# One first load of 65 KiB a row in two descriptors, in place of loads of 8 and 57 KiB: x + alpha * fx

## The chip, the cores and the metric

The kernel runs on one core of one Trainium2 chip. The metric is device time in microseconds, as the median of repeated runs; the kernel before takes 151.0 us (three runs, 150.94 to 151.18). A separate execution is recorded by the hardware profiler, and all views of the profile tell of that one.

## The reference

```python
B, S, D = 512, 32, 640            # all bf16; alpha has one element
def reference(x, fx, alpha):
    return x + alpha * fx
```

Two tensors of 20 MiB (20.97 MB) are read, one of the same size is written. Per element there is one multiply and one add.

## The kernel before, in words

**Tiling.** Each tensor is seen as 128 partition rows of 160 KiB (`ROW = 160`, in units of `K = 512` bf16 elements, which are 1 KiB). All work is told in KiB of a row: "x 0 64" is the first 64 KiB of each of the 128 rows. On the chip there is one flat buffer `t`, 128 partitions of 160 + 47.5 KiB. x lies in it at its own place, 0 to 160, and the result overwrites x there. There is not room for all of fx beside it: fx passes through places that are free for a while, the part of x's own space that has not been loaded yet (95 to 160) and the spare 47.5 KiB (160 to 207.5).

**The steps.** `PLAN` (lines 27 to 54) is the order of work, written out by hand, one step to a line; nothing reorders it. There are these kinds:

- `x a b` loads x from a to b (`load_x`, line 96), `f a b p` loads fx from a to b into place p (`load_f`, line 100), `a` loads alpha (`load_alpha`, lines 103 to 110), `s a b` stores the result (`store`, line 119). All of these are issued by SyncE (SP), into one DMA queue that the 16 DMA engines work off in order.
- `m a b` multiplies fx by alpha in place on VectorE (DVE) (line 113), and `c a b` adds it to x (line 116), also on DVE.

Alpha is loaded into eight partitions; a matmul with a row of ones (line 108) spreads one of them over 128 partitions, and DVE copies it from PSUM to `a_f` (line 110), which all multiplies read.

**What sets the order around the change.** Each engine does its own steps in the order of `PLAN`. Between engines, semaphores carry the data's dependencies: a multiply waits for its fx load, an add for its x load, a load into a place waits until what lay there has been used. So the load "x 95 160" (line 39) is issued only when the adds on fx 0 to 65, which lies in 95 to 160, are over; "f 112.5 142.5" and "f 142.5 160" wait in the same way for the adds over 65 to 95 and 95 to 112.5. The first store is held until "m 112.5 134.5" is over (line 47), and the others follow the adds. A last instruction of SP waits for all but the last store.

**Descriptors.** A load of 128 rows becomes one packet for each contiguous piece of a row, eight rows to each of the 16 DMA engines. Rows of 8, 57, 64, 31, 47.5, 30 and 17.5 KiB go in one piece; the rows of 65 KiB of "x 95 160" go in two of 32.5 KiB (128x2x16640 elements).

Of the kernel before, what the change touches and what calls it, by code (L numbers as in the profile page):

```python
# [1 line left out]

# [4 lines left out]

ALU = mybir.AluOpType
F32 = mybir.dt.float32

P = 128
K = 512
ROW = 160
SPARE = 47.5

LANES = 8

PLAN = """
f 0 8 95
a
f 8 65 103  # L30
x 0 64
x 64 95
f 65 112.5 160
m 0 8
m 8 65
c 0 8
c 8 64
c 64 65
x 95 160
m 65 95  # L40
c 65 95
f 112.5 142.5 160
m 95 112.5
c 95 112.5
f 142.5 160 190
m 112.5 134.5
s 0 64 | m 112.5 134.5
m 134.5 142.5
c 112.5 142.5
m 142.5 160  # L50
c 142.5 160
s 64 128
s 128 160
"""


@with_exitstack
def kernel(
    ctx: ExitStack,
    tc: tile.TileContext,  # L60
    x: bass.AP,
    fx: bass.AP,
    alpha: bass.AP,
    out: bass.AP,
):
    nc = tc.nc
    xv, fv, ov = (
        t.flatten_outer_dims().rearrange("(p n) d -> p (n d)", p=P) for t in (x, fx, out)
    )
    assert xv.shape[1] == ROW * K  # L70

    consts = ctx.enter_context(tc.tile_pool(name="consts", bufs=1))
    psum = ctx.enter_context(tc.tile_pool(name="psum", bufs=1, space=bass.MemoryType.PSUM))
    flat = ctx.enter_context(tc.tile_pool(name="flat", bufs=1))
    ctx.enter_context(tc.manual_schedule())
    t = flat.tile([P, int((ROW + SPARE) * K)], x.dtype, name="t")
    info = mybir.DependencyInfo(mybir.DependencyClass.Sync, mybir.DependencyReason.DATA)

    lanes = {}
    lies = []  # L80
    done = []

    def at(a, b):
        return t[:, int(a * K) : int(b * K)]

    def of(v, a, b):
        return v[:, int(a * K) : int(b * K)]

    def place(a, b):
        for c, d, p in reversed(lies):  # L90
            if c <= a and b <= d:
                return at(p + a - c, p + b - c)
        raise ValueError(f"fx {a} to {b} lies nowhere in one piece")

    def load_x(a, b):
        done.append(nc.sync.dma_start(out=at(a, b), in_=of(xv, a, b)))

    def load_f(a, b, p):
        lies.append((a, b, p))
        done.append(nc.sync.dma_start(out=at(p, p + b - a), in_=of(fv, a, b)))  # L100

    def load_alpha():
        a_n = consts.tile([LANES, 1], alpha.dtype, name="a_n")
        done.append(nc.sync.dma_start(out=a_n[:], in_=alpha[None, :].to_broadcast([LANES, 1])))  # L104
        ones = consts.tile([1, P], alpha.dtype, name="ones")
        nc.vector.memset(ones[:], 1.0)  # L106
        a_ps = psum.tile([P, 1], F32, name="a_ps")
        done.append(nc.tensor.matmul(a_ps[:], ones[:], a_n[0:1, :], start=True, stop=True))  # L108
        lanes["a"] = consts.tile([P, 1], F32, name="a_f")
        nc.vector.tensor_copy(out=lanes["a"][:], in_=a_ps[:])  # L110

    def multiply(a, b):
        done.append(nc.vector.tensor_scalar_mul(place(a, b), place(a, b), lanes["a"][:]))  # L113

    def add(a, b):
        done.append(nc.vector.tensor_add(at(a, b), at(a, b), place(a, b)))  # L116

    def store(a, b):
        done.append(nc.sync.dma_start(out=of(ov, a, b), in_=at(a, b)))

    does = {"x": load_x, "f": load_f, "a": load_alpha, "m": multiply, "c": add, "s": store}
    begun = {}
    for step in filter(None, PLAN.split("\n")):
        step, *later = step.split(" | ")
        what, *numbers = step.split()
        does[what](*map(float, numbers))
        begun[step] = done[-1]
        for other in later:
            tc.add_manual_dep(done[-1].ins, begun[other].ins.name, info, reason="begins late")

    rest = nc.sync.nop(nofuse=True)
    for i in done[:-1]:
        tc.add_manual_dep(rest.ins, i.ins.name, info, reason="all but the last store")


# [1 line left out]
_INS = ['x', 'fx', 'alpha']  # L137
_OUTS = [((512, 32, 640), 'bfloat16')]


# [23 lines left out]
```

## Time and profile before

| | |
|---|---|
| median of 3 runs | 151.0 us (150.94 to 151.18) |
| the profiled execution's own time | 151.11 us |
| its span, first to last instruction | 149.3 us |
| DMA queue | 1728 packets, 62.92 MB, 98.0% of 16 engines |
| mean rate over the span | 421 GB/s |
| DVE busy | 66.5 us (45%), 16 instructions |
| adds (line 116) | 43.6 us in 7 |
| multiplies (line 113) | 22.8 us in 7 |
| DVE idle ahead of multiplies, waiting for fx | 25.7 us in 3 waits, the longest 15.3 |
| DVE idle ahead of adds, waiting for x | 16.5 us in 2 waits, the longest 11.6 |

How to read it: "busy" is the time in which an engine works, and the idle time of an engine that is not the bottleneck costs nothing. The DMA share of the queue is the mean over the 16 DMA engines. In the chain of waits each step is followed back to what released it; "another core or an unknown queue" is a release that the profile could not put a name to. A landing is the moment at which a transfer's completion is seen by the engine that waits for it. In the windows a packet is counted whole in the window in which it starts, so a short window can show a share over 1.

### The profile page before, as it was taken

What the parts mean: (1) busy time and instruction counts of PE and PEld (TensorE: products, weight loads), DVE (VectorE), ACT (ScalarE), POOL (GpSimd) and SP (SyncE); (2) the same over time, 40 slices, a digit from 0 to 9 for tenths busy, and PEclk for the clock granted to TensorE, in tenths of its full rate; (3) what the DMA queues carried; (4) which work ended last, traced back from release to release, by engine and by line L of the source; (5) the groups of instructions that cost most, each with busy time, mean ns of one, the idle gap of its engine ahead of it and who ended that gap; (6) DMA issues with size and microseconds to landing.
All of it is one profiled execution on the core that took longest, in us unless ns stands there. A gap on an engine that the chain in (4) does not pass through costs nothing.

```text
span 149.3 us, 84 instructions
## 1 busy us (share of the span) xinstructions
PE 0.2 (0%) x1; PEld 0.1 (0%) x1; DVE 66.5 (45%) x16; POOL 0.2 (0%) x4
## 2 busy tenths in 40 slices
PE   0000000000000000000000000000000000000000
PEld 0000000000000000000000000000000000000000
DVE  0300008920069999029997093599997000000000
POOL 0000000000000000000000000000000000000000
DMA  5969998969699999999999999899896969697993
GB/s 147 603 281 500 500 461 351 562 281 562 281 408 451 438 417 443 456 429 428 428 428 428 417 444 469 378 526 492 351 562 281 562 281 562 281 562 307 456 474 167
DMA packets 1728, 62.92 MB, mean 421 GB/s; under 512 B 192, under 2 KB 192, under 8 KB 192
## 3 DMA queue, kind: packets, MB, share of 16 engines
q1 hardware_dynamic: 1728, 62.92, 98.0%
HBM read 41.94 MB, written 20.97 MB: 421 GB/s over the span
## 4 chain that ended last, share of the span: by engine, by line
DMA 38%; DVE 33%; another core or an unknown queue 4%; SPq 1%; issue 0%; DVEq 0%
DMA t<-in_x_dram 27%; DVE t L116 26%; DMA t<-in_fx_dram 11%; DVE t L113 7%; SPq L100 0%; SPq L104 0%; DVEq L116 0%
## 5 line engine op out<-in xcount | busy, mean ns | idle before, releaser
L116 DVE TENSOR_TENSOR t<-t 128x15360 bf16<-128x15360 bf16 (+4 forms) x7 | 43.6, 6252 | 16.6 <-DMA t<-in_x_dram 16.5
L113 DVE TENSOR_SCALAR t<-t,a_f 128x4096 bf16<-128x4096 bf16 (+4 forms) x7 | 22.8, 3265 | 25.7 <-DMA t<-in_fx_dram 25.7
L110 DVE COPY a_f<-a_ps 128x1 f32<-128x1 f32 x1 | 0.2, 159 | 5.2 <-PE a_ps L108 5.2
L106 DVE MEMSET ones<- 1x128 bf16 x1 | 0.2, 165 | 0.8 <-PEq L148 0.8
L108 PE MATMUL a_ps<-a_n,ones 1*128 1x1 bf16 x1 | 0.2, 158 | 6.0 <-DMA a_n<-in_alpha_dram 6.0
L148 POOL MEMSET const-bfloat16-1.0<- 128x1 bf16 x1 | 0.1, 102 | 0.0
L148 POOL MEMSET const-uint8-127<- 128x1 uint8 x1 | 0.1, 102 | 0.0
L148 POOL MEMSET const-float32-1.0<- 128x1 f32 x1 | 0.1, 99 | 0.0
L108 PEld LDWEIGHTS <-ones 1*128 1x128 bf16 x1 | 0.1, 98 | 1.0 <-DVE ones L106 1.0
L148 POOL MEMSET const-float32-0.0<- 128x1 f32 x1 | 0.1, 98 | 0.2 <-issue 0.2
## 6 DMA issues: line engine op xcount, KB each, us to landing
t<-in_x_dram SPq DMA_DIRECT2D x1, 8320.0 KB, 25.8
t<-in_fx_dram SPq DMA_DIRECT2D x1, 7296.0 KB, 21.4
t<-in_fx_dram SPq DMA_DIRECT2D x1, 6080.0 KB, 63.0
out_dram<-t SPq DMA_DIRECT2D x1, 4096.0 KB, 33.7
t<-in_x_dram SPq DMA_DIRECT2D x1, 3968.0 KB, 49.3
t<-in_fx_dram SPq DMA_DIRECT2D x1, 3840.0 KB, 16.4
t<-in_fx_dram SPq DMA_DIRECT2D x1, 2240.0 KB, 9.5
t<-in_fx_dram SPq DMA_DIRECT2D x1, 1024.0 KB, 5.0
```

The source lines that it names most:

```text
L106: nc.vector.memset(ones[:], 1.0)
L108: done.append(nc.tensor.matmul(a_ps[:], ones[:], a_n[0:1, :], start=True, stop=True))
L110: nc.vector.tensor_copy(out=lanes["a"][:], in_=a_ps[:])
L113: done.append(nc.vector.tensor_scalar_mul(place(a, b), place(a, b), lanes["a"][:]))
L116: done.append(nc.vector.tensor_add(at(a, b), at(a, b), place(a, b)))
L148: nc = _bacc.Bacc("TRN2", target_bir_lowering=False, num_devices=1)
```

## The change

Two loads of fx, the first 8 KiB of each row and then the next 57, become one load of 65 KiB a row. Such a row goes as two descriptors of 32.5 KiB, in the shape that "x 95 160" already has. It still lies at 95 to 160 of the buffer. There are seven loads of x and fx instead of eight. Alpha's load, which stood between the two, now follows the one. The multiplies over 0 to 8 and 8 to 65 become one over 0 to 65, and the adds over 0 to 8 and 8 to 64 one over 0 to 64; the add over 64 to 65 stays.

```diff
 PLAN = """
-f 0 8 95
+f 0 65 95
 a
-f 8 65 103
 x 0 64
 x 64 95
 f 65 112.5 160
-m 0 8
-m 8 65
-c 0 8
-c 8 64
+m 0 65
+c 0 64
 c 64 65
 x 95 160
 m 65 95
```

Nothing else differs. On each engine the remaining instructions stand in the same order: DVE has 14 in place of 16 (without its branches), SP one load fewer, and what later instructions wait for is the same data as before.

## The prediction

> **What bounds the kernel now.** I read the page's slices first, then the queue, the chain of waits, the timeline of VectorE (DVE), SyncE's (SP's) timeline, and last the windows over the first microseconds.
>
> ```profile
> DMA  5969998969699999999999999899896969697993
> q1 hardware_dynamic: 1728, 62.92, 98.0%
> ```
>
> The 16 DMA engines are busy for 98.0% of the span, and the dips in the slices are packets counted whole in the slice they start in. The bound is therefore bytes: 62.92 MB through 16 engines. The chain, in order of time:
>
> ```profile
> 1.59 0.35 SPq L100
> 1.94 0.04 issue
> 1.98 40.34 DMA t<-in_x_dram
> ...
> 42.41 17.63 DVE t L116 x3
> 60.04 6.08 another core or an unknown queue
> 66.12 0.02 issue
> 66.14 4.23 DVE t L113
> ```
>
> It runs through DVE from 42.41 to 60.04, but the 6.08 us behind that show that DVE did not set the pace there: the load issued at 60.07 was queued behind fx 65 to 112.5, which landed only at 66.12. What the reader is to see: queued loads land one behind the other without a hole. First multiplies and adds on DVE, whose starts are those landings, and SP's issues:
>
> ```profile
> 0.73 0.38 SPq L100 DMA_DIRECT2D t<-in_fx_dram  x1
> 5.97 0.16 PE L108 MATMUL a_ps<-a_n,ones 1*128 1x1 bf16 x1 [5.97 <-DMA a_n<-in_alpha_dram]
> 22.99 7.82 DVE L113 TENSOR_SCALAR t<-t,a_f 128x29184 bf16<-128x29184 bf16 x1 [15.34 <-DMA t<-in_fx_dram]
> 60.07 0.38 SPq L96 DMA_DIRECT2D t<-in_x_dram  x1
> 85.94 4.83 DVE L116 TENSOR_TENSOR t<-t 128x8960 bf16<-128x8960 bf16 x1 [4.91 <-DMA t<-in_x_dram]
> ```
>
> Only the start is not at full rate. Of these windows only the last two columns matter here, the DMA share and GB/s. A packet is counted whole where it starts, so GB/s over share is the rate of an engine while busy (times 16), and share times window times 16 is the packets' own time.
>
> ```profile
> 1.70:2.10 0.40, 0.00 (x0) 0.00 (x0) 0.00 (x0) 0.00 (x0) 1.00 2.08 287
> 2.10:2.30 0.20, 0.00 (x0) 0.00 (x0) 0.00 (x0) 0.00 (x0) 1.00 0.00 0
> 2.30:2.60 0.30, 0.00 (x0) 0.00 (x0) 0.00 (x0) 0.00 (x0) 1.00 0.15 55
> 3.40:4.80 1.40, 0.00 (x0) 0.00 (x0) 0.00 (x0) 0.00 (x0) 1.00 0.97 410
> 6.90:7.60 0.70, 0.00 (x0) 0.00 (x0) 0.70 (x1) 0.00 (x0) 1.00 3.08 1334
> 5.50:22.00 16.50, 0.16 (x1) 0.00 (x0) 1.45 (x2) 0.00 (x0) 1.00 0.91 396
> 66.00:84.50 18.50, 0.00 (x0) 0.00 (x0) 14.84 (x3) 0.00 (x0) 1.00 1.00 432
> ```
>
> In 1.70 to 2.10 start 287 x 0.40 = 115 KB, 14 packets of 8 KiB, of 2.08 x 0.40 x 16 / 14 = 0.95 us each; from 3.40 on one takes 0.31 us (8192 B at 410/0.97 = 423 GB/s over 16). So 14 engines begin at once and each loses some 0.64 us on its first packet; the other two begin only after 2.30. In 6.90 to 7.60 all 16 engines start a 57 KiB packet (1334 x 0.70 = 934 KB), each their second; one takes 58368 B at 396/0.91 = 435 GB/s, 2.15 us, so the first ones started between 4.75 and 5.45. Eight packets of 0.31 us from 1.75 on would have ended at 4.23: **the start costs each engine 0.5 to 1.2 us, and the kernel ends by the last engine.**
>
> **The change, part by part.** The profiled execution took 151.11 us, 1.8 around its span of 149.3, and is 0.11 above the median of 151.0.
>
> *Bytes and packets.* Per partition row 8 + 57 KiB become 32.5 + 32.5 KiB: the same bytes, and 256 descriptors either way. Before: 1.049 MB at 423 and 7.471 MB at 435 GB/s, 2.48 + 17.17 = 19.65 us. After: if the new row runs at the full 435, 8.520 MB take 19.59 (-0.07). The nearest row by shape is the load of x 95 to 160, two descriptors of 32.5 KiB too: 85.94 - 66.14 = 19.80 us (+0.15). That load ran beside 14.84 us of DVE work in 18.5 us; the first load will run beside none. I take 0, bounds -0.07 and +0.15.
>
> *One load fewer in the queue.* If a queued load had a fixed price, short ones would land late for their size. fx 112.5 to 142.5 (30 KiB a row) landed at 94.95, 9.01 after the one ahead, 0.300 us a KiB; x 0 to 64 took 42.32 - 22.99 = 19.33, 0.302 a KiB. The short one is not dearer, so in the queue the price is about nothing. Alone, a load does have one:
>
> ```profile
> t<-in_fx_dram SPq DMA_DIRECT2D x1, 1024.0 KB, 5.0
> ```
>
> The first load needs 5.0 us from issue to landing, 2.5 over the 2.48 of its bytes. I take 0, the queue's row, as every load but the first is queued; the bounds are 0 and -2.5. The Trainium skill, "DMA: Bandwidth & Descriptors", section "Anatomy of one DMA — SWDGE (gpsimd) path", fits a transfer as some 2.0 us fixed plus its bytes; by that figure, paid one behind the other, the sum would be 149.0. The section is for another issuing engine; the first load's row agrees with such a cost, the landings in the queue show it hidden.
>
> *SP.* One issue (0.35 us and 0.04 behind it) goes; alpha's stays at 1.17, and x 0 to 64, x 64 to 95 and fx 65 to 112.5 are issued 0.39 us sooner. The engines need x 0 to 64 only at about 22, so this is worth nothing.
>
> *Alpha, and DVE's multiplies.* Alpha's few bytes are now queued behind 65 instead of 8 KiB a row, so they land at about 23.0 and not 5.97. From alpha's landing to the first multiply it takes 6.36 - 5.97 = 0.39 us (matmul, copy). The two multiplies (1.29 + 7.82) become one of 33280 columns: 7.82 plus 4096 columns at (7.82 - 4.22)/(29184 - 15360) = 0.26 ns, 8.89 us. It starts at some 23.4 to 23.7 and ends by 32.6. Nothing else is queued behind it on DVE but the add that waits for x, landing at 42.32: 9.7 us of cover. If that were gone, each us would delay x 95 to 160, with the slack that comes next.
>
> *DVE's adds.* 2.29 + 15.09 become one of 32768 columns: 15.09 + 4096 x (15.09 - 8.16)/(28672 - 15360) = 17.22 us, 0.16 less. SP issues x 95 to 160 at about 59.9 and not 60.07. From SP's first issue at 0.73 to the first packets in the window from 1.70 are 1.0 us, so that the descriptors stand ready at 61, and the queue ahead lands at 66.12: some 4 us of slack, and the 0.16 us buys nothing. The later links (issues at 78.58, 90.79, 98.15) keep their distances, as they hang on landings.
>
> *The start itself.* The first packet of an engine is 32.5 KiB, not 8. Trace and kernel show no start of that shape. Best case: only the first packet's loss (0.64 us in the mean) is left, what the last engine lost on its next packets is covered, 1.2 - 0.64 = -0.56. Worst case: 16 descriptors for an engine instead of 8 take twice as long to come; the last engine began between 2.30 and 2.70 (0.6 to 0.95 behind the first), twice that is 1.2 to 1.9, against 1.2 lost now: up to +0.7. The nearest row is the same addresses' start, as all engines read the same first bytes of the same rows: I take 0.
>
> Sum: 0 + 0 + 0 on 151.11, less the 0.11 to the median: **151.0 us.**
>
> **The rivals.**
>
> *Faster: the ramp's later losses go (150.45).* Speaks for it: between 2.60 and the steady 0.31 us the engines still lose, and with 1.2 us of bytes in each packet an engine has its next descriptor long before it needs it. [...] 151.0 - 0.56 = 150.45.
>
> *Slower: descriptors come later (151.5).* Place: SP's first issue, with 256 descriptors ahead of the first byte of the last engines. For it: two of 16 engines began over 0.5 us behind the others, and the issues that follow rise from 0.35 to 0.51 us each, as if something behind SP were full. It decides once the last engine begins over 1.2 us behind the first, at about 2.95; doubled offsets give 0 to 0.7 more, in the middle 0.35, and with the +0.15 of the row rate 151.5. Against: the only such load took SP 0.38 us (60.07), as long as the first load of 128 descriptors. The Trainium skill, "Perfetto Trace Analysis", section "DMA Instruction — HWDGE (DVE, Sync)", puts the making of descriptors inside that time, and by it all would stand ready before the first packet; that leaves the time at 151.0.
>
> *No effect for another reason: DVE.* The late alpha takes the place of a wait; it decides only beyond 9.7 us. 151.0.
>
> *Much faster: each load pays the first one's 2.5 us (148.5).* 151.0 - 2.5, if the queue hid nothing of it. The landings in the queue, with no 2.5 us between a short and a long load, speak against it.
>
> **How the numbers follow.** This kernel's runs differ by 0.24 us, so 0.2% (0.3 us) is about what can be told from none. Forecast, no change, 0.48 (its own range 150.7 to 151.3); with the two-descriptor row at its worst, +0.15, 0.02; ramp gains 0.20; fixed cost 0.02; late descriptors 0.28. So faster 0.22, same 0.50, slower 0.28. The range goes from 150.4 (the ramp's gain in full) to 151.7 (+0.7 on the last engine).
>
> **What would show it.** Right: 14 or more engines begin at about 1.7 to 2.1, the add after fx 0 to 65 starts at 42.4 plus or minus 0.3, its multiply at 23.4 to 23.7, the last add and the last store keep their distance to it, and the span is 149.0 to 149.6. The faster rival shows as x 0 to 64 landing by 42.0 or sooner, the slower one as packets of 32.5 KiB that first start after 2.95 and a landing after 42.6. Wrong would be any hole in the DMA share behind the first load, or a wait of DVE on alpha that reaches 42.

## The result and the profile after

The changed kernel takes 151.63 us (median of 7 runs, 151.4 to 151.71) against 151.13 for the kernel before in the same comparison: a ratio of 1.0032, with a 95% interval of 1.0023 to 1.0042. It is 0.5 us slower. The forecast was no change, at 151.0.

The profiled execution took 151.66 us, with a span of 149.9; the one before took 151.11, with 149.3. The page's slices and its queue line, in the kernel after:

```profile
DMA  5999999989699999999999999999796969898993
q1 hardware_dynamic: 1712, 62.92, 97.8%
```

The bytes are the same, the packets fewer by 16, all of them under 512 bytes (176 in place of 192), and the queue is as full as it was. Nothing opened in the middle. The timeline of the kernel after, from SP's first issue to the second load of x:

```profile
0.73 0.43 SPq L97 DMA_DIRECT2D t<-in_fx_dram  x1
23.43 0.16 PE L105 MATMUL a_ps<-a_n,ones 1*128 1x1 bf16 x1 [23.43 <-DMA a_n<-in_alpha_dram]
23.82 8.89 DVE L110 TENSOR_SCALAR t<-t,a_f 128x33280 bf16<-128x33280 bf16 x1
42.77 17.23 DVE L113 TENSOR_TENSOR t<-t 128x32768 bf16<-128x32768 bf16 x1 [10.06 <-DMA t<-in_x_dram]
60.36 0.38 SPq L93 DMA_DIRECT2D t<-in_x_dram  x1
66.51 4.22 DVE L110 TENSOR_SCALAR t<-t,a_f 128x15360 bf16<-128x15360 bf16 x1 [6.18 <-DMA t<-in_fx_dram]
```

Alpha lands at 23.43, the multiply takes 8.89 us, and DVE then sits idle for 10.06 us until x 0 to 64 lands: the cover that was counted on is there. But that landing comes at 42.77 instead of 42.41, 0.36 us late, and the steps on DVE that follow keep their distance to it (66.51 is 0.37 later than 66.14). So this much of the loss lies ahead of 42.77. The two executions differ by more, 0.55 us in their own times; what comes behind 42.77 in them is taken up below, where x 95 to 160 is loaded in two. The windows of the kernel after over the first microseconds and over the rest of the first load (last two columns: DMA share and GB/s; packets counted where they start):

```profile
1.70:2.10 0.40, 0.00 (x0) 0.00 (x0) 0.00 (x0) 0.00 (x0) 1.00 3.85 915
2.10:2.60 0.50, 0.00 (x0) 0.00 (x0) 0.00 (x0) 0.00 (x0) 1.00 1.04 333
2.60:3.00 0.40, 0.00 (x0) 0.00 (x0) 0.00 (x0) 0.00 (x0) 1.00 0.00 0
5.50:21.50 16.00, 0.00 (x0) 0.00 (x0) 0.00 (x0) 0.00 (x0) 1.00 1.00 433
```

915 x 0.40 / 33.28 = 11 packets of 32.5 KiB start by 2.10, and 333 x 0.50 / 33.28 = 5 by 2.60: all 16 engines have begun by 2.60, 11 of them by 2.10, where it was 14 in the kernel before. Together these first packets hold (3.85 x 0.40 + 1.04 x 0.50) x 16 = 33 us, 2.06 each. Later on one takes 33280 B at 433 GB/s over 16, 1.23 us. **The loss on the first packet is 0.83 us in the mean of all engines.** With packets of 8 KiB it was 0.64 for the 14 that began early and next to nothing for the other two, some 0.57 in the mean of 16. The 11 that begin early here lose 3.85 x 0.40 x 16 / 11 - 1.23 = 1.01 us each. Behind it the row of two descriptors runs at 433 GB/s.

The kernel ends by its last engine, and that one can be found too. These are windows in which the last engines begin their next packet, first of the kernel before (the first packet of 57 KiB), then of the kernel after (the second of 32.5 KiB):

```profile
5.40:5.50 0.10, 0.00 (x0) 0.00 (x0) 0.00 (x0) 0.00 (x0) 1.00 1.35 584
5.50:6.80 1.30, 0.16 (x1) 0.00 (x0) 0.60 (x2) 0.00 (x0) 1.00 0.00 0
```

```profile
4.50:4.60 0.10, 0.00 (x0) 0.00 (x0) 0.00 (x0) 0.00 (x0) 1.00 0.77 333
4.60:5.00 0.40, 0.00 (x0) 0.00 (x0) 0.00 (x0) 0.00 (x0) 1.00 0.00 0
```

In each pair one packet begins in the first window and none in the second. Before, the last engine is through with its eight packets of 8 KiB at about 5.45; at the steady 0.31 us each they are 2.48 us, so it stands as if it had begun at 2.97. After, the last one is through with its first packet at about 4.55, 1.23 us of steady work, as if it had begun at 3.32. That is 0.35 us later, as much as x 0 to 64 lands late.

### The profile page after: what moved, and what is told of

It reads as the page before. It is cut to its first block, busy times and chain, and to the rows that moved or that the text cites. A ratio compares the mean times of both kernels' runs of the same rounds, so it can differ in the third digit from the quotient of the medians.

```text
span 149.9 us, 81 instructions
## 1 busy us (share of the span) xinstructions
PE 0.2 (0%) x1; PEld 0.1 (0%) x1; DVE 66.2 (44%) x14; POOL 0.2 (0%) x4
## 4 chain that ended last, share of the span: by engine, by line
DMA 38%; DVE 33%; another core or an unknown queue 4%; SPq 1%; issue 0%; DVEq 0%
DMA t<-in_x_dram 27%; DVE t L113 26%; DMA t<-in_fx_dram 11%; DVE t L110 7%; SPq L97 0%; SPq L101 0%; DVEq L113 0%
## 5 line engine op out<-in xcount | busy, mean ns | idle before, releaser
L113 DVE TENSOR_TENSOR t<-t 128x15360 bf16<-128x15360 bf16 (+3 forms) x6 | 43.5, 7268 | 15.1 <-DMA t<-in_x_dram 15.0
L110 DVE TENSOR_SCALAR t<-t,a_f 128x8960 bf16<-128x8960 bf16 (+4 forms) x6 | 22.5, 3772 | 10.4 <-DMA t<-in_fx_dram 10.4
L105 PE MATMUL a_ps<-a_n,ones 1*128 1x1 bf16 x1 | 0.2, 158 | 23.4 <-DMA a_n<-in_alpha_dram 23.4
```

## The experiments

All ratios are to the kernel before, run in turn on the same chip. "The add" is the one that waits for x 0 to 64; its start is the landing of that load, and so the time at which the last engine is through with the first 65 KiB of fx and x 0 to 64. In the profile of before it starts at 42.41.

### Loads or DVE?

The first kernel has the loads of before and the DVE steps of after; the second the reverse.

```diff
 f 0 8 95
 a
 f 8 65 103
-m 0 8
-m 8 65
-c 0 8
-c 8 64
+m 0 65
+c 0 64
```

> Loads as before (8, then 57 KiB a row), multiply and add as in the changed kernel (one over 0 to 65, one over 0 to 64). If the 0.5 us come from the first load, size or count of its descriptors: as before, within 0.15 us of it. If they come from the multiply that now starts late, or from the merged add: 0.4 to 0.6 us slower.

Measured: 151.02 us, 1.0001 (0.9992 to 1.0010), the add at 42.31.

```diff
 f 0 65 95
 a
-m 0 65
-c 0 64
+m 0 8
+m 8 65
+c 0 8
+c 8 64
```

> The one load of 65 KiB of the changed kernel, with the multiplies (0 to 8, 8 to 65) and adds (0 to 8, 8 to 64) of before. If the first load costs it: 0.4 to 0.6 us slower than before, x 0 to 64 landing some 0.35 us later. If DVE costs it: as before.

Measured: 151.56 us, 1.0031 (1.0020 to 1.0042), the add at 42.75. The load makes the whole difference; DVE none that can be told, within 0.15 us.

### Descriptors' size or number?

Two loads of 32.5 KiB a row (large packets, 8 descriptors for an engine), and a first load of two pieces of 8 KiB of each row (small packets, 16 descriptors). Both have the DVE steps of after, as have all the kernels below that split the first 65 KiB.

```diff
-f 0 65 95
+f 0 32.5 95
 a
+f 32.5 65 127.5
```

> Two loads of 32.5 KiB a row with alpha between them, one multiply, one add: the packets of the changed kernel, but 8 descriptors for an engine in the first load, as before, and not 16. Theory of size (a large first packet loses more): 0.3 to 0.6 us slower than before, the first packets some 1.0 us longer than the steady 1.23. Rival, count (16 descriptors take longer to come): as before within 0.15 us.

Measured: 151.29 us, 1.0014 (1.0006 to 1.0023), the add at 42.37.

```diff
-f 0 65 95
-a
+g 0 65 95 0 8       # of both halves of each row, the first 8 KiB
+a
+g 0 65 95 8 32.5    # the other 24.5 KiB of both
...
+        def of_halves(v):
+            return v.rearrange("p (h n) -> p h n", h=2)[:, :, int(c * K) : int(d * K)]
```

> The first load takes two pieces of 8 KiB of each row (at 0 and at 32.5), the second the two other pieces of 24.5 KiB; one multiply, one add: 16 descriptors for an engine in the first load, as in the changed kernel, but small first packets, as before. Theory of size: as before within 0.2 us. Rival, count: 0.3 to 0.6 us slower than before, late first packets.

Measured: 151.31 us, 1.0016 (1.0007 to 1.0025), the add at 42.60. Half of the loss with each, so neither theory holds as it stands. The second has excuses: SP's issue of a load in two pieces a row takes 0.43 us and not 0.38, and it has 16 more packets for each engine, at up to 9 ns (8 KiB at 423 instead of 435 GB/s), together up to 0.19 us of its 0.24 to 0.28.

### A late start of another load?

In the profile of after, one more thing stood out. The load of fx 142.5 to 160 is issued at 91.15, some 3 us before the engines come to it, and some of its first packets were slow. A window of the kernel after:

```profile
94.00:94.60 0.60, 0.00 (x0) 0.00 (x0) 0.00 (x0) 0.00 (x0) 1.00 0.93 329
```

329 / 0.93 is 354 GB/s instead of 435. Both kernels were run with x 95 to 160 in two loads, so that fx 142.5 to 160 can be issued at about 86.

```diff
-x 95 160
+x 95 112.5
+x 112.5 160
```

> The kernel before with x 95 to 160 loaded in two (17.5 and 47.5 KiB a row), so that the add over 95 to 112.5 is done earlier and fx 142.5 to 160 is issued some 8 us instead of 3 ahead of need. If the late first packets of that load (0.3 to 0.5 us on two engines in the profile of before, 1.0 on one in the profile after) come from a short lead, they vanish here; the time stays within 0.15 us of before, as the two engines were the earliest. If they come by chance, they stay.

Measured: 151.07 us, 0.9996 (0.9986 to 1.0005), the add at 42.27.

> The changed kernel with the same split of x 95 to 160. If the 0.5 us are the start's loss alone: still 0.5 slower than before, and x 0 to 64 lands some 0.3 later than before. If a part is the late first packets of fx 142.5 to 160, on an engine that then ends last: 0.2 to 0.35 slower.

Measured: 151.60 us, 1.0033 (1.0023 to 1.0043), the add at 42.74. The windows of this second kernel, the change with x split:

```profile
1.70:2.10 0.40, 0.00 (x0) 0.00 (x0) 0.00 (x0) 0.00 (x0) 1.00 5.15 1331
2.10:2.60 0.50, 0.00 (x0) 0.00 (x0) 0.00 (x0) 0.00 (x0) 1.00 0.00 0
94.00:94.60 0.60, 0.00 (x0) 0.00 (x0) 0.00 (x0) 0.00 (x0) 1.00 0.99 418
```

The slow packets at 94 are gone (418 / 0.99 = 422 GB/s), and the time is 0.5 us longer all the same: the loss comes from the start. In the two profiled executions with the split the add is 0.47 us later and the time 0.43 longer (151.43 against 151.00). In those of before and after without it, it was 0.36 at the add and 0.55 in the time, so some 0.2 us came behind the add there. The slow packets at 94 lie in that stretch; that they made those 0.2 us is not shown. The first two lines show more. Here all 16 engines begin within 0.4 us (1331 x 0.40 / 33.28 = 16), and still a first packet takes 5.15 x 0.40 = 2.06 us. **No engine began late; the first packets themselves are slow.** The same split with two loads of 32.5 KiB tells where their half loss lies:

> Two loads of 32.5 KiB a row, with x 95 to 160 loaded in 17.5 and 47.5 KiB, so that no first packet of fx 142.5 to 160 is late. If the 0.2 us of the two loads of 32.5 came from late packets behind the start (its add over x 0 to 64 started at 42.37, as before): within 0.1 us of before. If from the start: 0.15 to 0.3 us slower.

Measured: 151.29 us, 1.0013 (1.0004 to 1.0021), the add at 42.59. Without late packets the same 0.25 us remain, and here they are at the start. In the profile without the split the add stood at 42.37, as before, and that execution still took 151.27 us: its loss came behind the add, where two packets of fx 142.5 to 160 took 0.94 and 1.04 us instead of 0.67. One execution each does not tell how often it goes one way or the other.

### How much the first load takes of a row

```diff
-f 0 8 95
+f 0 1 95
 a
-f 8 65 103
+f 1 65 96
```

> First load 1 KiB a row, then alpha, then 64 KiB a row; one multiply, one add. Theory of size (the larger the first packets, the more is lost at the start): as before or up to 0.2 us faster. Rival (16 descriptors for an engine, and of large packets, are what is late; 8 of any size are not): as before within 0.15 us, less the price of eight small packets.

Measured: 152.11 us, 1.0060 (1.0042 to 1.0078), the add at 43.36. Its windows, with 1 KiB first:

```profile
1.70:2.50 0.80, 0.00 (x0) 0.00 (x0) 0.00 (x0) 0.00 (x0) 1.00 0.62 164
2.50:3.00 0.50, 0.05 (x1) 0.00 (x0) 0.00 (x0) 0.00 (x0) 1.00 5.74 1835
```

164 x 0.80 is the whole first load, 128 packets of 1 KiB, and the next packets begin at 2.50 or later: the engines ran dry, and then the 64 KiB packets made a start of their own. Both theories missed this; neither had counted the second load's issue at 1.59. The other sizes have the same edit with other numbers:

> First load 4 KiB a row, then alpha, then 61 KiB a row; one multiply, one add. Its packets last some 1.3 us with the first one's delay 2, and the second load is issued 0.86 us after it, so no engine should run dry as it did with 1 KiB. If smaller is better at the start: 0.05 to 0.2 us faster than before, the add over x 0 to 64 at 42.1 to 42.3. If the second load's large packets lose as a first load's do: slower by 0.2 to 0.5.

Measured: 151.14 us, 1.0017 (0.9998 to 1.0036; 150.84 to 152.35 in its runs), the add at 42.38. Nothing is gained over 8 KiB; whether a little is lost can't be told.

> First load 16 KiB a row, then alpha, then 49 KiB a row; one multiply, one add. If the loss grows with the stretch or size of the first load: between before and the load of 32.5 KiB (which cost 0.2), so 0 to 0.2 us slower. If it is a matter of 16 descriptors or of more than 32.5 KiB: as before.

Measured: 151.05 us, 1.0002 (0.9994 to 1.0011), the add at 42.29.

> First load 48 KiB a row in one descriptor, then alpha, then 17 KiB a row; one multiply, one add. If the loss grows with the bytes of the first load: between 32.5 (0 to 0.2) and 64 KiB (0.46), so 0.2 to 0.45 us slower, the add over x 0 to 64 at 42.45 to 42.75. If it is a threshold above 48: as before.

Measured: 151.44 us, 1.0025 (1.0014 to 1.0036), the add at 42.87.

> First load 64 KiB a row in one descriptor each, then alpha, then the remaining 1 KiB a row; one multiply, one add. Theory of size: 0.4 to 0.8 us slower than before, as the first packets are twice those of the changed kernel. Rival (16 descriptors for an engine): as before within 0.15 us.

Measured: 151.53 us, 1.0031 (1.0020 to 1.0042), the add at 42.85. The windows of this kernel, 64 KiB in one descriptor first:

```profile
1.70:2.10 0.40, 0.00 (x0) 0.00 (x0) 0.00 (x0) 0.00 (x0) 1.00 6.85 2130
2.10:2.60 0.50, 0.00 (x0) 0.00 (x0) 0.00 (x0) 0.00 (x0) 1.00 1.09 393
```

Here 13 and 3 engines begin, with packets of (6.85 x 0.40 + 1.09 x 0.50) = 3.29 us in the mean, against 65536 B at 435 GB/s over 16, 2.41: 0.87 lost, the same as with two descriptors of 32.5 KiB. Eight descriptors for an engine lose as much as sixteen. The loss grows with what the first load takes of a row: none that can be told at 4, 8 and 16 KiB, 0.25 us at 32.5, 0.4 at 48, 0.5 at 64 and 65. The intervals of neighbouring sizes overlap; the trend from 16 to 64 KiB is clear of them.

### Is it the descriptor, the load, or the place in memory?

Two pieces of 28 KiB, and four of 14, of each row, the rest in the second load, as in the kernel with two pieces of 8:

```diff
-g 0 65 95 0 8
+g 0 65 95 0 28
 a
-g 0 65 95 8 32.5
+g 0 65 95 28 32.5
```

> First load two pieces of 28 KiB of each row (at 0 and 32.5), second load the two pieces of 4.5 KiB left; one multiply, one add. 16 large descriptors for an engine in the first load, as in the changed kernel, but not one stretch of a row. Theory of count (16 large descriptors in one load): 0.4 to 0.6 us slower than before, the add over x 0 to 64 starting at 42.7 or later. Rival, the stretch (32.5 + 32.5 and 64 KiB are slow since an engine reads one long stretch of a row before the next row): 0.1 to 0.3 us slower (16 more packets at some 5 ns, and SP's longer issue), the add at 42.4 to 42.6.

Measured: 151.59 us, 1.0038 (1.0025 to 1.0051), the add at 42.83.

> First load four pieces of 14 KiB of each row (every 16.25), second load the four pieces of 2.25 KiB left; one multiply, one add. An engine stays in a row as long as in the changed kernel, with small packets. By rows alone 48 more packets an engine at some 5 ns and SP's longer issue cost 0.3 us. Theory of the stretch (time an engine stays in one row at the start): 0.6 to 0.8 us slower than before, the add over x 0 to 64 at 42.9 or later. Rival, size of the packets (28 KiB and more): 0.25 to 0.4 us slower, the add at 42.6 to 42.7.

Measured: 151.86 us, 1.0053 (1.0041 to 1.0066), the add at 43.28. Of its 0.8 us up to 0.48 are 48 more packets for each engine (9 ns) and the issue; at least 0.3 remain, with packets smaller than the 16 KiB that lost nothing. Its first windows show the loss itself:

```profile
1.70:2.10 0.40, 0.00 (x0) 0.00 (x0) 0.00 (x0) 0.00 (x0) 1.00 2.79 430
2.10:2.80 0.70, 0.00 (x0) 0.00 (x0) 0.00 (x0) 0.00 (x0) 1.00 0.26 82
```

These are 12 and 4 first packets of 14 KiB, of 2.79 x 0.40 + 0.26 x 0.70 = 1.30 us in the mean, against 14336 B at 435 GB/s over 16, 0.53: 0.77 lost, nearly the 0.83 of the kernel after. So the descriptor's size doesn't decide either; what this kernel has in common with the slow ones is the 56 KiB that the first load takes of a row.

Then the two halves of a row's piece were taken from places 80 and 48 KiB apart:

```diff
-f 0 65 95
+h 0 65 95 80        # and 48: halves at 0 and 80 (48) of each row
...
+        apart = of(fv, 0, 2 * q).rearrange("p (h n) -> p h n", h=2)[:, :, :h]
+        done.append(nc.sync.dma_start(out=halves, in_=apart))
```

> The changed kernel, its first load reading 0 to 32.5 and 80 to 112.5 KiB of each row of fx in place of 0 to 65, so the output is not the reference's there: 16 descriptors of 32.5 KiB for an engine as in the changed kernel, but an engine leaves the place after 32.5 KiB, as with two loads of 32.5. Theory of the stretch: 0.1 to 0.3 us slower than before, as the two loads of 32.5 were, the add over x 0 to 64 at 42.35 to 42.5. Rival, 16 large descriptors: 0.4 to 0.6 us slower, the add at 42.7 or later.

Measured: 151.71 us, 1.0042 (1.0028 to 1.0055), the add at 43.11. SP's first issue took 0.64 us here, and no packet began before 2.10, so 0.3 of it is a late issue. With 48 KiB the issue is short:

> The changed kernel, its first load reading 0 to 32.5 and 48 to 80.5 KiB of each row of fx, so the output is not the reference's there. The reading of 80 KiB apart was muddled by an issue that took SP 0.21 us longer. If 16 large descriptors in a load lose, wherever the second half lies: 0.4 to 0.6 us slower than before, the add at 42.7 or later, with an issue of some 0.43. If the unbroken stretch of a row is what loses: 0.1 to 0.3 us slower, the add at 42.35 to 42.5.

Measured: 151.53 us, 1.0031 (1.0020 to 1.0042), the add at 42.83, the issue 0.44. An unbroken stretch isn't needed: the same loss with a hole of 15.5 KiB in each row.

Last, the rows' distance in memory. The first load reads one whole piece of fx, in rows 65 KiB apart instead of 160, once as in the changed kernel and once with one descriptor of 64 KiB a row:

```diff
-f 0 65 95
+h 0 65 95
...
+        packed = flat_f[: P * n].rearrange("(p n) -> p n", p=P)
+        done.append(nc.sync.dma_start(out=at(p, p + b - a), in_=packed))
```

> The changed kernel, its first load reading the first 8.52 MB of fx in one piece (rows 65 KiB apart in memory instead of 160), so the output is not the reference's in those columns; two descriptors of 32.5 KiB a row as before. If the loss at the start comes of the distance of the rows in memory (engines that start side by side in the same places): 0.2 us or more of the 0.5 go. If it comes of the descriptors: 0.4 to 0.6 us slower than before, the add over x 0 to 64 at 42.7 or later.

Measured: 151.29 us, 1.0014 (1.0005 to 1.0023), the add at 42.38. Its windows:

```profile
1.70:2.10 0.40, 0.00 (x0) 0.00 (x0) 0.00 (x0) 0.00 (x0) 1.00 3.34 915
2.10:2.60 0.50, 0.00 (x0) 0.00 (x0) 0.00 (x0) 0.00 (x0) 1.00 1.03 333
```

The counts of packets are those of the kernel after to the digit (11 and 5), the descriptors and their sizes too; a packet takes 3.34 x 0.40 + 1.03 x 0.50 = 1.85 us instead of 2.06. The last engines begin their second packet sooner:

```profile
4.10:4.20 0.10, 0.00 (x0) 0.00 (x0) 0.00 (x0) 0.00 (x0) 1.00 1.54 666
4.20:4.80 0.60, 0.00 (x0) 0.00 (x0) 0.00 (x0) 0.00 (x0) 1.00 0.00 0
```

That is by 4.20 instead of 4.60, and the add comes 0.39 us sooner too. This execution, at 151.11 us, lies on the fast side of the median.

> The kernel whose first load is 64 KiB a row in one descriptor, but reading rows that lie 65 KiB apart in memory, so the output is not the reference's there. If the distance of the rows decides, whatever the descriptors (two of 32.5 KiB lost 0.3 of their 0.5 us so): 0 to 0.25 us slower than before instead of 0.46, the add over x 0 to 64 at 42.3 to 42.5. If a first packet of 64 KiB is itself slow: 0.4 to 0.6 us slower, the add at 42.75 or later.

Measured: 151.25 us, 1.0013 (1.0004 to 1.0022), the add at 42.48 instead of 42.85. With either form some 0.26 us, about half of the loss, go when the rows lie closer (0.0018 of the ratio each time, known to about 0.0014). The rows' distance is not all that changes with it: the load then reads one block of 8.5 MB instead of places spread over the whole of fx. The Trainium skill, "DMA: Bandwidth & Descriptors", section "Latency and other measured facts", tells of copies whose rate falls where the rows' distance in memory is a large power of two, from 512 KiB on, and comes back with 4 KiB of padding; it calls its explanation by memory channels an inference. Neither 160 nor 65 KiB is such a distance, and behind the start the kernel after moves 433 GB/s, so these runs neither bear that row out nor contradict it. They show a loss at the start alone that goes with where the rows lie, and not the mechanism.

None of these kernels beats the one before; the first loads of 4 and 16 KiB and that of 8 KiB with x split can't be told from it.

## Why the prediction was wrong, point by point

- **What bounds the kernel** held: bytes through a queue without a hole. What the last engine lost at the start was still there at the end (0.5 us in the medians); in the two profiled executions it was 0.36 at the add and 0.55 in their times.
- **Bytes and packets** held at 0: behind the start the two-descriptor row ran at 433 GB/s.
- **One load fewer** held: nothing of the order of 2 us was gained. A gain of a few hundredths inside the 0.5 us of loss can't be told.
- **Alpha and DVE** held nearly to the digit: multiply at 23.82 (told 23.4 to 23.7, without the late start), 8.89 us long (told 8.89), 10.06 us of cover (told 9.7), and the exchange of the DVE steps alone moved nothing that can be told.
- **The start itself** is the step that failed. It took 0 "as all engines read the same first bytes of the same rows". They do, for the first 8 KiB; but the first packets lose 0.83 us in the mean instead of some 0.57, and the last engine is 0.36 to 0.47 us later at the add (42.77 and 42.74 against 42.41 and 42.27). The term should have been about +0.5 us, which is the whole difference in the medians. I had put the row nearest in address ahead of the fact that nothing in the trace of before shows a start with more than 8 KiB of a row. The bound of +0.7 held it by luck: it was worked out for descriptors that come late, and none did.
- **The slower rival** had the right time (151.5) by luck, for mostly the wrong reason. One of its signs came, a landing after 42.6. Its mechanism did not: descriptors were to come late, with the last engine beginning after 2.95. All began by 2.60, with x split all by 2.10, and 64 KiB in 8 descriptors lost as much. The +0.15 of the row rate did not come either (433 GB/s). Some 0.05 us is real: the issue takes 0.43 instead of 0.38, the first packets begin that much later.
- **The faster rival** fell: the last engine lost more in its first packet of 32.5 KiB than in the whole start before (as if begun at 3.32 against 2.97).

What is shown: the loss comes from the first load and not from DVE; it lies in the first packets and in the last engine to be through with them; and it goes with how much of a row the first load takes, whatever the number and size of the descriptors. That about half of it goes with the place of the rows in memory rests on two pairs of kernels. What stays open: in all these kernels "the bytes of the first load" and "how long an engine stays in its first row before it goes to the next" change together, since an engine has eight rows in every load; and the rows' distance was not changed apart from the size of the block that is read. That engines which stay in rows 160 KiB apart hinder each other until they have drifted apart would fit these runs, but it was only argued. The remaining 0.2 us with rows 65 KiB apart (0.05 of it the issue, in the form with two descriptors) are also not explained.

## What to carry to other kernels

In a kernel bound by a full DMA queue, look at the first packets and at the last engine, in windows of some tenths of a microsecond; here the 0.5 us came from there. The start was best with a first load that takes a little of every row (4 to 16 KiB here), so that it lasts until the second load's packets can begin; with 1 KiB the engines ran dry, and with 32.5 KiB and more the start got slower. Try such sizes in another kernel; these runs show them for rows 160 KiB apart only. When a trace shows no start of the shape that a change brings, the nearest row by address or by size is a guess, and its price should be taken between the bounds rather than at one end.

## What the runs showed that I had not expected

- A load's first packets, with the queue empty ahead of it, took some 0.6 to 0.9 us longer than the same packets later, in the mean of the 16 engines and in the kernels whose windows are shown. By how much went with the rows' place in memory (2.06 us against 1.85 for 32.5 KiB, with rows 160 and 65 KiB apart).
- A load that is issued 3 us before the engines reach it, behind a full queue, can still have slow first packets (354 GB/s in the window at 94.00); issued 8 us ahead, it had none in the three kernels with x split. Of the 17 profiles with the short lead, 13 have packets of that load that take over 0.72 us instead of 0.67, and four have none. They cost nothing measurable in the kernel before, 0.9996 without them.
- SP's issue of a first load with two pieces a row is 0.05 us longer (0.43 against 0.38), and in one case, pieces 80 KiB apart, 0.26 longer (0.64), which at the start of the queue is paid in full. It is not so for every such load: x 95 to 160, two pieces a row too, took 0.38 at 60.36.
